# Attention routing on a second PSUM bank and at other places, states stored in another order, and eight zero products per iteration

## The chip, the cores and the metric

The kernel runs on one core of a Trainium2 chip. The metric is the device time of one execution in microseconds. Five engines work side by side, each through its own list of instructions in order: PE (TensorE, with its weight loads shown as PEld), DVE (VectorE), ACT (ScalarE), POOL (GpSimd) and SP (which here only issues DMAs). They wait for one another through semaphores.

## The reference

Three layers in a row. The first is a gated linear attention over 4 batches, 8 heads, 768 positions and a head size of 48, the second a top-1 mixture of 8 experts over the resulting 3072 tokens, the third a gated feed-forward layer:

```
for t in range(S):
    state = alpha[:, :, t, :, None] * state + k_t (outer) v_t
    y[:, :, t] = q_t @ state
logits = x @ w_gate;  expert = argmax(logits)
out[token] = gate[token] * (relu(x @ w1[expert]) @ w2[expert])
h = out @ w_in;  result = (h * sigmoid(h)) @ w_out
```

## The kernel before

**Attention.** Two heads of a batch form a pair; there are 16 pairs (0 to 15), four to a batch, and the main loop runs over the pairs `p`, one iteration each, and once more for the tail of the last pair. The 768 positions are cut into 6 chunks of 128. In iteration `p` PE computes, in this order:

- the scores of pair `p` (`scores`, tile Ap, PSUM banks 0 and 1);
- transposes of the scaled keys (`ks_transpose`, tile Tp, bank 2), four chunks, and two more later; ACT copies each lot out to kst;
- the part of the output of pair `p - 1` that comes from its states (`from_states`, tile Yp, banks 5 and 6), which reads the states So;
- the chunk updates of the state (`updates`, tiles U in bank 3 and, for half chunks, Ue in bank 4);
- between the two the part of the output within a chunk (`within`, into Yp).

DVE runs two long decay scans (Pf at L570, Rv at L588), masks the scores (Am, L621), scales the keys (L593), and in `states` scans U into the running states (run, L654) and adds Ue into So (L664); ACT copies the rest of So (L663). `from_states` of the next iteration needs both.

**Routing.** When the four pairs of a batch are done, the tokens of that batch are routed beside the following pairs. The steps are: the gate's logits (Lp), a turn (Lt), the choice of an expert and its weight (small DVE steps), ranks within the expert (`ranks`, pp), slots, six turned blocks of rows (`rows`, tile Xt: four PE transposes, then two ACT activations at L955 that scale by the gate weight into xr, and every second block a store to DRAM), and the inverse list (`hots` on DVE, `invert`, tile pt, on PE, `add` on DVE). All PSUM tiles of the routing come from `xbank()`, which in the attention gives bank 7 and only that; each of them therefore waits until the one before it has been read out.

**What sets the order.** The program is written under a manual schedule: each engine runs its instructions in the order in which the code issues them. `aside(p, place)` issues the routing steps that a hand-written table (`beside_pairs`) has put at a place of iteration `p`. The places in order are A (behind the scores), F1 and F2 (ahead of `from_states`), F3 (behind the second lot of key transposes), U (ahead of the updates), C1 (behind `states`) and C2. Routing of batch 0 lies beside pairs 5 to 10, that of batch 1 beside 9 to 14, that of batch 2 beside 13 to 15, and that of batch 3 behind the attention, beside the first expert tiles.

**Warming.** In iterations 0 to 4 some products on a tile of zeros (`warm`, tile Lw, L543, 256 columns each) run on PE beside the real ones; later iterations have none.

**Behind the attention** come the expert products and the last layer, where PE runs without a pause.

Of the kernel before, what the change touches and what calls it, by code (L numbers as in the profile page):

```python
# [23 lines left out]
PA = 112  # L24
CH = 128
# [215 lines left out]
def gla_moe_kernel(  # L241
# [164 lines left out]
    with actx:  # L406
# [127 lines left out]
        constants()  # L534
        U = bank(3, [PA, D, NC], "U")
        nc.vector.memset(U, 0.0)
        Ue = bank(4, [PA, NC, D], "Ue")
        nc.vector.memset(Ue, 0.0)
        Lw = bank(7, [128, 256], "Lw")

# [96 lines left out]
        def updates(p, n):  # L637
            s = st[p]
            for c in range(NC - 1 if n == CH else NC):
                for h in range(2):  # L640
                    r = slice(64 * h, 64 * h + D)
                    nc.tensor.matmul(
                        U[r, :, c + 1] if n == CH else Ue[r, c, :],
                        lhsT=s["kst"][:n, c, r],
                        rhs=s["v"][:n, (h * NC + c) * D : (h * NC + c + 1) * D],
                        start=True,
                        stop=True,
                    )

        def states(p):  # L650

            so = So[p % 2]
            run = wk.tile([PA, D, NC], F32, tag="run", name="run")
            nc.vector.tensor_tensor_scan(  # L654
                run.rearrange("p e c -> p (e c)"),
                U.rearrange("p e c -> p (e c)"),
                st[p]["W"],
                0.0,
                op0=ALU.add,
                op1=ALU.mult,  # L660
            )
            by_c = run.rearrange("p e c -> p c e")
            nc.scalar.copy(so[:, D:NS].rearrange("p (c e) -> p c e", e=D), by_c[:, 1:NC])  # L663
            nc.vector.tensor_tensor(so[:, NS : 2 * NS].rearrange("p (c e) -> p c e", e=D), by_c, Ue, op=ALU.add)  # L664

        xb = {}

# [4 lines left out]
        def from_states(p):  # L672

            s = st[p]
            s["y"] = y = [bank(5 + h, [128, NC, HC], "Yp") for h in range(2)]
            new = set()
            for c in range(NC):
                for u in range(2):
                    for h in range(2):
                        if c or u:  # L680
                            r, z = slice(64 * h, 64 * h + D), slice(u * HC, u * HC + HC)
                            o, w = half(h, u), (u * NC + c) * D
                            s["mm"] = nc.tensor.matmul(
                                y[h][o : o + 64, c, :],
                                lhsT=So[p % 2][r, w : w + 64],
                                rhs=s["qs"][r, c, z],
                                start=(h, u) not in new,
                                stop=False,
                            )
                            new.add((h, u))  # L690
# [37 lines left out]
        XB = [0]  # L728

        XBS = [7]  # L730

        def xbank():
            XB[0] += 1
            return XBS[XB[0] % len(XBS)]

# [255 lines left out]
        def beside_pairs(b):  # L991
            s_, tb = route(b)
            digits, hots, invert, add = tb
            row = [lambda c=c: rows(b, c) for c in range(NC)]
            p = 4 * b + 5
            at = {
                (p, "A"): [lambda: logits(b), s_["l_copy"]],
                (p, "F2"): [s_["l_turn"]],
                (p, "F3"): [s_["l_rows"], *s_["choose"][:2], s_["w_exp"]],
            }  # L1000
            if b < B - 2:
                at |= {
                    (p, "C1"): s_["choose"][2:] + [s_["w_gate"]],
                    (p + 1, "F2"): [s_["ranks"]],
                    (p + 1, "C1"): s_["slots"],
                    (p + 1, "C2"): [digits],
                    (p + 2, "F2"): [row[0]],
                    (p + 2, "F3"): [row[1]],
                    (p + 3, "F1"): [row[2]],
                    (p + 3, "F2"): [row[3]],  # L1010
                    (p + 3, "F3"): [row[4]],
                    (p + 4, "F1"): [row[5], hots],
                    (p + 5, "F1"): [invert, add],
                }
            else:
                at |= {
                    (p, "C1"): s_["choose"][2:] + [s_["w_gate"]],
                    (p + 1, "A"): [row[0], row[1]],
                    (p + 1, "F2"): [row[2]],
                    (p + 1, "F3"): [s_["ranks"], lambda: w_cast(2), lambda: w_cast(3)]  # L1020
                    + s_["slots"]
                    + [digits, lambda: w_rest(2), row[3], row[4]],
                    (p + 1, "U"): [row[5]],
                    (p + 1, "C1"): [hots],
                    (p + 2, "F2"): [invert, add, gather_a],
                    (p + 2, "C2"): [lambda: w_cast(0), lambda: w_cast(1), lambda: w_rest(3), lambda: w_rest(0), lambda: w_load(4)],
                }
            return at

        def aside(p, place):  # L1030
            for step in plan_r.get((p, place), []):
                step()
# [23 lines left out]
        for p in range(NP + 1):  # L1056
            on, oy = p < NP, p >= 1
            if on:
                begin(p)
                scores(p)  # L1060
            if p == 0:
                for t in [So[i][:, 2 * NS :] for i in range(2)] + [Es[NE][32:64]]:
                    nc.gpsimd.memset(t, 0.0)
            prepare(p, "head")

            aside(p, "A")
            if on:
                ks_transpose(p, 0, 4)
                if beside_scans(p):
                    mask_aside(p)  # L1070
            if p % 4 == 1 and 1 < p < NP:
                gather_last(p // 4)
            prepare(p, "scan")
            aside(p, "F1")
            if 1 <= p <= 4:
                warm(3)
            aside(p, "F2")
            if oy:
                from_states(p - 1)
            if on:  # L1080
                ks_transpose(p, 4, NC)
            else:
                st[p - 1]["mark"] = behind(nc.scalar.copy(wz[:, 0:1], wz[:, 1:2]), st[p - 1]["mm"])
            aside(p, "F3")
            if p == 0:
                warm(8)
            for T, i in work.get((p, "scan"), []):
                f(T, Q_SCALE)
                f(T, DECAY)
            aside(p, "U")  # L1090
            if not on:
                x_rows(XG[0], XS[0], 0, 0, 128, bank(2, [128, KD, 128], "xt"))
                x_rows(XG[1], XS[0], 1, 0, CA - 128, bank(0, [128, KD, 128], "xt"))
                w_rest(1)
            if on:
                updates(p, CH)
            if oy:
                within(p - 1)
            if oy:
                y_copy(p - 1, 0)  # L1100
                y_copy(p - 1, 1)
            if on:
                updates(p, HC)
                states(p)
            if p == 0:
                warm(22)
            aside(p, "C1")
            prepare(p, "end")
            if p == 1:
                nc.gpsimd.memset(wgs, 0.0)  # L1110
            if p == 2:
                for h in range(2):
                    for u in range(2):
                        z = wgs[half(h, u) : half(h, u) + D, h].rearrange("p i x -> p (i x)")
                        src = wg[64 * h : 64 * h + D].rearrange("p i x -> p (i x)")
                        nc.sync.dma_start(z[:, u * E :], src[:, 0 : 4 * 32 - u * E])
            if p == 5:
                more_constants()
            aside(p, "C2")
            if 1 <= p <= 3:  # L1120
                warm(3)
            if not on:
                logits(B - 1)
                last, last_tb = route(B - 1)
                last["l_copy"]()
                for t in range(5, 8):
                    w_load(t)
            if p + 1 in loads:
                load(loads[p + 1], "a")
            if p:  # L1130
                load_v(p + 2)
            if p + 1 in loads:
                load(loads[p + 1], "qk")
            if p >= 4 and p % 4 == 0 and p < NP:
                for at, todo in beside_pairs(p // 4 - 1).items():
                    plan_r[at] = plan_r.get(at, []) + todo
            if p in (11, 12):
                for t in range(2):
                    w_load(2 * (p - 11) + t)
# [591 lines left out]
```

## Time and profile before

| what | value |
| --- | --- |
| time, median of 3 runs | 796.06 us (795.36 to 797.17) |
| time of the profiled execution | 793.69 us |
| its span | 791.9 us |
| mean granted TensorE clock | 0.952 of full |
| busy share of PE, DVE, ACT, POOL | 96%, 59%, 45%, 19% |

The span is what the profile covers; the profiled execution's own time is 1.8 us longer. The attention lies in the first fifth of the span, so shares over the whole span say little about it; it has to be read by stretches of time. A granted clock of 1.00 is 2.4 GHz and of 0.50 is 1.2 GHz; values between are mixtures of the two in one stretch.

### The profile page before, as it was taken

The page shows a single profiled execution, that of the slowest core. Times are in us where ns is not written, and L with a number is a line of the kernel's source. Part 1 is how long each engine was busy: PE and PEld are TensorE (multiplying, and loading weights), DVE is VectorE, ACT ScalarE, POOL GpSimd, SP SyncE. Part 2 cuts the span into 40 slices and gives each one's busy share as a digit, 9 for nine tenths or more (in the row PEclk, how much of TensorE's full clock was granted, in tenths as well). Part 3 has the DMA queues.
Part 4 walks back from the last instruction along what each step waited for, and adds up shares of the span by engine and source line. Part 5 has one row for each costly group of instructions (what it writes and reads, how often), then busy time and mean ns, then how long its engine had stood idle before and what let it go on. Part 6 is the DMA issues. An engine that isn't in the chain of part 4 may idle for free. (4 is left out here: it accounts for less than half of the span.)

```text
span 791.9 us, 16908 instructions
## 1 busy us (share of the span) xinstructions
PE 756.9 (96%) x6730; PEld 692.2 (87%) x6730; DVE 468.4 (59%) x784; ACT 359.8 (45%) x691; POOL 152.4 (19%) x204
## 2 busy tenths in 40 slices
PE   8889787899999999999999999999999999999997
PEld 6668675779999999999998998989988999898996
DVE  8977775455678778888878533442333333344322
ACT  2334354343555554666644424554454545244222
POOL 5443341113043332311112120020010002002002
PEclk9976778588999999999999999999999999999999
DMA  9686974444366557666320120022012001001001
GB/s 247 166 204 173 218 218 111 110 107 154 126 193 192 177 173 205 198 185 190 122 81 21 36 75 18 1 75 52 3 38 72 19 18 41 2 0 41 1 1 43
DMA packets 41944, 81.25 MB, mean 103 GB/s; under 512 B 5840, under 2 KB 20127, under 8 KB 41832
## 3 DMA queue, kind: packets, MB, share of 16 engines
q1 hardware_dynamic: 37832, 67.64, 29.8%
q0 software_dynamic: 4000, 12.03, 5.1%
q8 instruction: 81, 1.33, 0.7%
q14 instruction: 31, 0.25, 0.1%
HBM read 68.08 MB, written 9.47 MB: 98 GB/s over the span
## 5 line engine op out<-in xcount | busy, mean ns | idle before, releaser
L1252 PE MATMUL hp<-xh,wh 128*128 128x512 f32 (+10 forms) x498 | 181.4, 366 | 1.0 <-ACT xh L378 1.0
L1252 PE MATMUL hp<-xh,wl 128*128 128x512 f32 (+10 forms) x498 | 180.9, 365 | 0.0
L1526 DVE TENSOR_TENSOR sg<-hp,sg 128x512 f32<-128x512 f32 (+1 forms) x97 | 66.5, 685 | 128.1 <-ACT sg L1525 127.6
L1252 PE MATMUL hp<-xl,wh 128*128 128x512 f32 (+10 forms) x498 | 127.4, 364 | 0.0
L1525 ACT ACTIVATE sg<-hp 128x512 f32<-128x512 f32 (+1 forms) x97 | 57.5, 593 | 118.1 <-PE hp L1252 113.3
L1252 PEld LDWEIGHTS hp<-xh,wh 128*128 128x128 f32 x498 | 94.7, 190 | 12.9 <-PE Lp L740 1.2
L1252 PEld LDWEIGHTS hp<-xh,wl 128*128 128x128 f32 x498 | 94.8, 190 | 10.5
L1252 PEld LDWEIGHTS hp<-xl,wh 128*128 128x128 f32 x498 | 90.5, 189 | 11.8
L1571 POOL DMA_INDIRECT out_dram<-o,sidx x24 | 23.3, 973 | 275.6 <-ACT o L1569 271.1
L1179 POOL TENSOR_TENSOR wl<-dx,wh 128x384 fp32r<-128x384 f32 x32 | 39.5, 1234 | 165.3 <-ACT wh L1176 165.3
L346 DVE TENSOR_TENSOR wl<-raw,wh 128x768 fp32r<-128x768 f32 x64 | 65.3, 1024 | 7.2 <-ACT wh L342 6.6
L1290 ACT ACTIVATE hh<-hp 128x464 fp32r<-128x464 f32 (+9 forms) x70 | 34.0, 487 | 75.3 <-PE hp L1252 68.4
L1292 DVE SCALAR_TENSOR_TENSOR hl<-hp,hh 128x464 fp32r<-128x464 f32 (+9 forms) x70 | 38.0, 549 | 29.8 <-ACT hh L1290 29.5
L1537 DVE TENSOR_TENSOR hl<-sg,hh 128x512 fp32r<-128x512 f32 x49 | 33.9, 692 | 35.9 <-ACT hh L1536 34.5
L342 ACT CAST wh<-raw 128x768 fp32r<-128x768 f32 x64 | 51.9, 832 | 6.1 <-DMA raw<-in_wt_dram 5.8
L1536 ACT CAST hh<-sg 128x512 fp32r<-128x512 f32 x49 | 30.4, 621 | 50.1 <-DVE sg L1526 38.4
L1537 DVE TENSOR_TENSOR xl<-sg,xh 128x512 fp32r<-128x512 f32 (+1 forms) x48 | 32.7, 681 | 31.7 <-ACT xh L1536 21.3
L1342 PE MATMUL both<-hh,wh 128*128 128x396 f32 (+9 forms) x140 | 47.8, 341 | 0.0
L1342 PE MATMUL both<-hl,wh 128*128 128x396 f32 (+9 forms) x140 | 46.1, 329 | 0.1
L1342 PE MATMUL both<-hh,wl 128*128 128x396 f32 (+9 forms) x140 | 45.9, 328 | 0.0
L1536 ACT CAST xh<-sg 128x512 fp32r<-128x512 f32 (+1 forms) x48 | 29.3, 611 | 35.1 <-DVE sg L1526 32.0
L364 POOL DMA_INDIRECT xg<-x_d,gidx x29 | 33.4, 1152 | 54.2 <-PE hp L1252 23.6
(335 smaller groups left out, 1580.4 us busy)
## 6 DMA issues: line engine op xcount, KB each, us to landing
raw<-in_wt_dram SPq DMA_DIRECT2D x64, 384.0 KB
raw<-in_w_dram SPq DMA_DIRECT2D x32, 384.0 KB
raw<-in_alpha_dram SPq DMA_DIRECT2D x16, 336.0 KB
x_d<-xr SPq DMA_DIRECT2D x24, 192.0 KB
E<-in_q_dram SPq DMA_DIRECT2D x18, 144.0 KB
E<-in_k_dram SPq DMA_DIRECT2D x18, 144.0 KB
E<-E POOLq DMA_DIRECT2D x18, 114.0 KB
E<-in_q_dram SPq DMA_DIRECT2D x4, 336.0 KB
```

The costliest lines, as they stand in the source:

```text
L342: nc.scalar.copy(wslot[slot1(t)][0], raw[t])
L346: eng.tensor_tensor(lo, raw.pop(t), hi.bitcast(F32), op=ALU.subtract)
L364: nc.gpsimd.indirect_dma_start(out=x[:n], out_offset=None, in_=src, in_offset=bass.IndirectOffsetOnAxis(ap=idx[:n, i : i + 1], axis=0),)
L1179: nc.gpsimd.tensor_tensor(r["lo"], r["x"], r["hi"].bitcast(F32), op=ALU.subtract)
L1252: nc.tensor.matmul(hp, lhsT=a[:, kc * 128 : (kc + 1) * 128], rhs=x[:, kc, c0:c1], start=(i == 0), stop=(i == 8))
L1290: nc.scalar.activation(hh[:, :n], hp, AF.Relu)
L1292: nc.vector.scalar_tensor_tensor(hl[:, :n], in0=hp, scalar=0.0, in1=hh[:, :n].bitcast(F32), op0=ALU.max, op1=ALU.subtract)
L1342: nc.tensor.matmul(yb[dc][:, c0:c1], lhsT=a[:, c : c + 128], rhs=b_[:, : c1 - c0], start=(f == 0 and c0 == 0 and i == 0), stop=(f == NF - ...
L1525: nc.scalar.activation(sg[:, z], hp[:, z], AF.Sigmoid)
L1526: nc.vector.tensor_tensor(sg[:, z], hp[:, z], sg[:, z], op=ALU.mult)
L1536: nc.scalar.copy(hh[:, z], sg[:, z])
L1537: nc.vector.tensor_tensor(hl[:, z], sg[:, z], hh[:, z].bitcast(F32), op=ALU.subtract)
```

## The change

Three things are edited.

1. `lent` is a list of banks that `xbank()` hands out first. The table puts `two(2)`, which lends bank 2 (that of the key transposes Tp), ahead of some steps at place U. The table itself puts the row blocks, `ranks`, `l_turn`, `hots`, `invert` and `add` at other places; a place C0, right behind `states`, is new.
2. Ue is laid out with the chunk innermost, as U is. `states` now reads run in its own order and writes So with a step of 48 numbers, where before it read run with a step of 6 numbers and wrote So in order. What So holds and how `from_states` reads it is as before.
3. `from_states` issues eight products of 128 x 128 on the tile of zeros, into columns of bank 5 that nothing else uses, ahead of its own products. It runs 16 times.

```diff
-        Ue = bank(4, [PA, NC, D], "Ue")
+        Ue = bank(4, [PA, D, NC], "Ue")
...
-                        U[r, :, c + 1] if n == CH else Ue[r, c, :],
+                        U[r, :, c + 1] if n == CH else Ue[r, :, c],
...
-            by_c = run.rearrange("p e c -> p c e")
-            nc.scalar.copy(so[:, D:NS].rearrange("p (c e) -> p c e", e=D), by_c[:, 1:NC])
-            nc.vector.tensor_tensor(so[:, NS : 2 * NS].rearrange("p (c e) -> p c e", e=D), by_c, Ue, op=ALU.add)
+            nc.scalar.copy(so[:, D:NS].rearrange("p (c e) -> p e c", e=D), run[:, :, 1:NC])
+            nc.vector.tensor_tensor(so[:, NS : 2 * NS].rearrange("p (c e) -> p e c", e=D), run, Ue, op=ALU.add)
...
-            s["y"] = y = [bank(5 + h, [128, NC, HC], "Yp") for h in range(2)]
+            t = [bank(5 + h, [128, 512], "Yp") for h in range(2)]
+            s["y"] = y = [x[:, 0 : NC * HC].rearrange("p (c t) -> p c t", c=NC) for x in t]
+            for _ in range(8):
+                nc.tensor.matmul(t[0][:, NC * HC :], lhsT=wz[:, 0:128], rhs=wz[:, 0:128], start=True, stop=True)
...
+        lent = []
...
+            if lent:
+                return lent.pop(0)
             XB[0] += 1
             return XBS[XB[0] % len(XBS)]
...
-                (p, "F2"): [s_["l_turn"]],
-                (p, "F3"): [s_["l_rows"], *s_["choose"][:2], s_["w_exp"]],
+                (p, "F3"): [s_["l_turn"], s_["l_rows"], *s_["choose"][:2], s_["w_exp"]],
...
+            two = lent.append
...
-                    (p + 2, "F2"): [row[0]],
-                    (p + 2, "F3"): [row[1]],
-                    (p + 3, "F1"): [row[2]],
-                    (p + 3, "F2"): [row[3]],
-                    (p + 3, "F3"): [row[4]],
-                    (p + 4, "F1"): [row[5], hots],
-                    (p + 5, "F1"): [invert, add],
+                    (p + 2, "A"): [row[1]],
+                    (p + 2, "F3"): [row[2]],
+                    (p + 2, "U"): [lambda: two(2), row[3]],
+                    (p + 3, "A"): [row[4]],
+                    (p + 3, "F3"): [row[5]],
+                    (p + 4, "F1"): [hots],
+                    (p + 4, "U"): [lambda: two(2), invert],
+                    (p + 4, "C0"): [add],
...
+            aside(p, "C0")
             aside(p, "C1")
```

What this makes of PE's list in iteration 14 (beside which batch 2 is routed) is shown here. Xt x8 are two row blocks, x12 three; pt is `invert`, pp `ranks`, Yp at L683 `from_states`. Before, from the scores of pair 14 to its first updates:

```order
L616 MATMUL Ap<-E_139 64x64 x24
L944 MATMUL Xt<-ident,xb 128x112 x8
L603 MATMUL Tp<-ident,E_139 128x112 x4
L886 MATMUL pt<-rv,ol 128x32 x6
L944 MATMUL Xt<-ident,xb 128x112 x4
L683 MATMUL Yp<-E_138,So_172 64x64 x22
...
L944 MATMUL Xt<-ident,xb 128x112 x12
L642 MATMUL U<-v__2251,kst 48x48 x10
```

And in the change (`from_states` is at L685, the row blocks at L949, the zero products at L677):

```order
L616 MATMUL Ap<-E_139 64x64 x24
L949 MATMUL Xt<-ident,xb 128x112 x4
L603 MATMUL Tp<-ident,E_139 128x112 x4
L949 MATMUL Xt<-ident,xb 128x112 x4
L677 LDWEIGHTS wz
L677 MATMUL Yp<-wz 128x128
...
L685 MATMUL Yp<-E_138,So_172 64x64 x22
...
L949 MATMUL Xt<-ident,xb 128x112 x4
L642 MATMUL U<-v__2356,kst 48x48 x10
```

Of six row blocks ahead of the updates of pair 14 three are left; the others follow `states` and go into iteration 15, and `invert` of batch 1 has moved to iteration 13.

The second place is iteration 12 on PE, beside which rows of batch 1 are turned. Before:

```order
L616 MATMUL Ap<-E_137 64x64 x24
L603 MATMUL Tp<-ident,E_137 128x112 x4
L944 MATMUL Xt<-ident,xb 128x112 x8
L683 MATMUL Yp<-E_142,So_172 64x64 x22
L603 MATMUL Tp<-ident,E_137 128x112 x2
L944 MATMUL Xt<-ident,xb 128x112 x4
L642 MATMUL U<-v__1949,kst 48x48 x10
```

And in the change:

```order
L616 MATMUL Ap<-E_137 64x64 x24
L949 MATMUL Xt<-ident,xb 128x112 x4
L603 MATMUL Tp<-ident,E_137 128x112 x4
L677 LDWEIGHTS wz
L677 MATMUL Yp<-wz 128x128
...
L685 MATMUL Yp<-E_142,So_172 64x64 x22
L603 MATMUL Tp<-ident,E_137 128x112 x2
L949 MATMUL Xt<-ident,xb 128x112 x4
L642 MATMUL U<-v__2037,kst 48x48 x10
```

Where two blocks stood one behind the other ahead of `from_states`, one now stands ahead of the key transposes and one behind `from_states`, and the third has gone to iteration 11.

## Rows read from the trace of the kernel before

**Rows 1.** The page, the span in 40 slices: PE's busy tenths and granted clock.

```profile
PE   8889787899999999999999999999999999999997
PEclk9976778588999999999999999999999999999999
```

**Rows 2.** Windows by stage: length, busy per engine, clock, DMA share, GB/s.

```profile
10.00:161.50 151.50, 126.77 (x3271) 103.33 (x3269) 109.69 (x165) 63.52 (x146) 47.43 (x64) 0.78 0.68 178
200.00:787.40 587.40, 586.33 (x3120) 547.69 (x3118) 328.13 (x534) 278.29 (x504) 86.45 (x98) 1.00 0.26 80
```

**Rows 3.** Windows by iteration, 6 to 15: length, PE, PEld, DVE, ACT, POOL, clock, DMA.

```profile
56.00:65.00 9.00, 7.10 (x201) 6.13 (x199) 5.72 (x13) 3.09 (x8) 1.63 (x1) 0.73 0.81 204
65.00:74.00 9.00, 9.00 (x204) 8.12 (x202) 7.34 (x11) 4.16 (x10) 4.82 (x5) 0.51 0.71 182
74.00:80.70 6.70, 5.77 (x214) 5.09 (x210) 6.36 (x7) 4.62 (x13) 0.49 (x1) 1.00 0.50 129
80.70:88.70 8.00, 7.09 (x223) 5.09 (x219) 7.32 (x12) 3.89 (x11) 4.11 (x7) 1.00 0.90 205
88.70:101.20 12.50, 9.04 (x211) 8.21 (x207) 5.88 (x14) 3.00 (x8) 1.63 (x1) 0.59 0.91 232
101.20:107.50 6.30, 5.79 (x211) 4.82 (x205) 5.95 (x9) 3.27 (x9) 3.17 (x4) 1.00 0.63 186
107.50:118.00 10.50, 8.74 (x198) 7.70 (x200) 8.08 (x10) 5.87 (x15) 4.21 (x4) 0.68 0.79 226
118.00:126.20 8.20, 7.28 (x224) 5.29 (x220) 7.02 (x11) 3.48 (x9) 1.99 (x5) 0.99 0.80 195
126.20:144.30 18.10, 12.71 (x231) 10.55 (x227) 5.87 (x21) 8.73 (x22) 1.00 (x1) 0.65 0.32 82
144.30:154.20 9.90, 7.85 (x208) 6.90 (x204) 5.04 (x11) 3.36 (x8) 2.03 (x2) 0.67 0.31 91
```

**Rows 4.** Waits from 38 to 161 us: total, times, longest.

```profile
DVE run L654 <- PE U L642: 14.7, 8, 4.2
DVE So L664 <- PE Ue L642: 10.7, 10, 1.7
PE Xt L944 <- ACT xr L955: 6.4, 5, 2.0
PE Ap L616 <- issue: 2.5, 1, 2.5
```

**Rows 5.** Timeline of iterations 10, 12, 14: start, length, instruction, idle before.

```profile
95.94 0.20 PE L812 MATMUL pp<-oh,tri 128*128 128x48 bf16 x1 [0.96 <-DVE tab L892]
...
111.22 0.98 PE L944 MATMUL Xt<-ident,xb 112*128 112x112 f32 x4 [1.76 <-ACT xr L955]
...
129.73 0.60 PE L944 MATMUL Xt<-ident,xb 112*128 112x112 f32 x4 [1.97 <-ACT xr L955]
```

**Rows 6.** Groups of DVE by form: count, total us, mean ns, idle before.

```profile
L664 DVE TENSOR_TENSOR So<-run,Ue 112x288 f32<-112x288 f32 x16 | 10.9, 684 | 11.3 <-PE Ue L642 10.7
...
L573 DVE RECIPROCAL D<-Pf 128x6 f32<-128x6 f32 x9 | 1.7, 194 | 0.3
...
L781 DVE TENSOR_TENSOR oh<-w,fi 128x48 bf16<-128x48 f32 x3 | 1.0, 320 | 0.1
...
L836 DVE RECIPROCAL gt<-sm 128x6 f32<-128x6 f32 x4 | 0.8, 192 | 0.1
...
L775 DVE TENSOR_TENSOR eq<-eq,w 128x48 f32<-128x48 f32 x3 | 0.6, 208 | 0.1
...
L379 DVE TENSOR_TENSOR xl<-xt,xh 128x384 fp32r<-128x384 f32 x1 | 0.6, 557 | 1.1 <-ACT xh L378 1.1
```

**Rows 7.** Products into U and Ue in iteration 8: ns min/median/max, first and last start.

```profile
L642 PE MATMUL U<-v__1297,kst x20: 208/208/243, 78.9 to 79.4; 128*48 128x48 f32 x20
```

```profile
L642 PE MATMUL Ue<-v__1297,kst x24: 202/205/205, 80.2 to 80.7; 64*48 64x48 f32 x24
```

**Rows 8.** Timeline of the warming products of iteration 0.

```profile
15.04 2.58 PE L543 MATMUL Lw<-wz 128*128 128x256 bf16 x22
```

More of the change, by code (lines that the diff above doesn't have):

```diff
@@ L1003, in beside_pairs @@
                     (p, "C1"): s_["choose"][2:] + [s_["w_gate"]],
-                    (p + 1, "F2"): [s_["ranks"]],
+                    (p + 1, "F1"): [s_["ranks"]],
+                    (p + 1, "U"): [lambda: two(2), row[0]],
                     (p + 1, "C1"): s_["slots"],
                     (p + 1, "C2"): [digits],
-                    (p + 2, "F2"): [row[0]],
-                    (p + 2, "F3"): [row[1]],
-                    (p + 3, "F1"): [row[2]],
-                    (p + 3, "F2"): [row[3]],
-                    (p + 3, "F3"): [row[4]],
-                    (p + 4, "F1"): [row[5], hots],
-                    (p + 5, "F1"): [invert, add],
+                    (p + 2, "A"): [row[1]],
[6 more added lines that the diff above has]
+                    (p + 4, "C0"): [add],
                 }
@@ L1017, in beside_pairs @@
                     (p, "C1"): s_["choose"][2:] + [s_["w_gate"]],
-                    (p + 1, "A"): [row[0], row[1]],
-                    (p + 1, "F2"): [row[2]],
+                    (p + 1, "A"): [row[0]],
+                    (p + 1, "F2"): [row[1]],
                     (p + 1, "F3"): [s_["ranks"], lambda: w_cast(2), lambda: w_cast(3)]
                     + s_["slots"]
[L1022 to L1025, printed above, removed]
+                    + [digits, lambda: w_rest(2)],
+                    (p + 1, "U"): [lambda: two(2), row[2]],
+                    (p + 1, "C1"): [row[3], hots],
+                    (p + 2, "A"): [row[4]],
+                    (p + 2, "F2"): [row[5]],
+                    (p + 2, "F3"): [invert, add, gather_a],
                     (p + 2, "C2"): [lambda: w_cast(0), lambda: w_cast(1), lambda: w_rest(3), lambda: w_rest(0), lambda: w_load(4)],
```

## The prediction, made before the changed kernel was run

> **What bounds the kernel now.** I read the page's slices first [rows 1]: PE is at nine tenths from the ninth slice on, but its clock is below full in slices 3 to 10. So there are two stages. From 200 us on PE is busy 586.33 of 587.40 us at full clock [rows 2]; nothing of the change lies there, and what the attention gains or loses arrives at the end as it is. From 10 to 161.5 us PE is busy 126.77 us at a mean clock of 0.78 and DVE 109.69 us [rows 2]: neither is full, they wait for each other. The waits say how [rows 4]: DVE waited 14.7 us for the updates U and 10.7 us for Ue. DVE has its scans done and PE is late.
>
> The windows by iteration show when [rows 3]. At full clock an iteration takes 6.30 us (11), 6.70 (8), 8.00 (9) or 8.20 (13), and DVE is busy in 6 to 7 us of it: there DVE is the bound. Iteration 7, at 0.51 of the clock throughout, takes 9.00 us with PE busy in all of it: there PE is the bound. Three are longer: 10 with 12.50 us, 12 with 10.50 and 14 with 18.10, all with DVE below 8.1 us and a clock of 0.59 to 0.68. Ahead of each lies a PE pause: a wait of 2.5 us inside the scores of iteration 10 for nothing that the profile shows [rows 4], and 1.76 and 1.97 us in which row blocks wait until ACT has read the block before out of bank 7 [rows 5]. The clock then stands at half for several us.
>
> **The change part by part.**
>
> Row blocks and bank 2, iterations 14 and 15. Before, six blocks, `invert` and `ranks` use bank 7 one behind the other ahead of the updates of 14, and DVE stands 4.2 us for U [rows 4]. Now three blocks stand there, one of them on bank 2. What is left: iteration 11 with its two blocks is the model at full clock, 6.30 us [rows 3]. To it I add one wait, since the second block still waits until ACT has scaled the first, which waits for the gate weight (1.97 us before [rows 5], I take 1.5 as one block now lies ahead of it and not two), one more block (0.60 us [rows 5]), and the zero products (0.7, below): 9.1 us. At half clock I scale the model by 9.00 to 6.70, iteration 7 to iteration 8 [rows 3]: 11.2 us. So iteration 14 gains 6.9 to 9.0 us; I take 7.5. Iteration 15 takes over three blocks, 1.8 us and a wait or two for ACT between them, but has `invert` behind `from_states` and no longer ahead of it, and DVE is free there for 4.9 us (9.90 less 5.04 [rows 3]): +2 at half clock to -2 at full; I take -0.5.
>
> Iterations 10 and 12. In 10, `invert` of batch 0 and the 0.96 us for which `ranks` waited on DVE behind it [rows 5] go to iteration 9; a block comes in ahead of U: about -1 net, -5 if the 2.5 us pause does not come back and the clock stays up (12.50 against 8.00 with a margin). I take -2. In 12 the 1.76 us wait goes, and with it the clock's fall behind it: the iteration should come near DVE's 8.08 us of work [rows 3], -2 of a possible 2.4; the lower bound is 0, if the clock falls for another reason.
>
> What the moves cost elsewhere. `invert` now lies ahead of U in 9 and 13, on bank 2, behind `hots` on DVE: about 0.8 us for PE, by what iterations 9 and 13 (8.00 and 8.20 us long, DVE busy 7.32 and 7.02 [rows 3]) can hide 0.7 to 1.2; I take +0.5 each. Behind the waiting instruction stand U and then the scan into run on DVE. Blocks at U in 6, 7, 10, 11 and 14 must wait for ACT's copy of the second key lot out of bank 2. At U one block at full clock is 0.60 us, at half 0.98 [rows 5]; in 6 and 7 the clock is low and DVE waits, so up to 2 us are seen, while blocks no longer stand ahead of `from_states` there. I put 6 and 7 together at +0.5. Stores of the rows move with the blocks on SP's queue; the loads queued behind them have the DMA engines at 0.31 to 0.91 of their time [rows 3], and I cost this at nothing while an iteration of lead remains; without it, the loads set the pace (a rival below).
>
> States. DVE's add into So takes 684 ns for 288 elements [rows 6]; the nearest addition that reads PSUM and has everything in order is 384 elements in 557 ns [rows 6], which gives 0.42 us for 288 by proportion, or 0.46 if the 0.19 us of a 6-element row [rows 6] is what an instruction costs at any size. Now the reads are in order and the writes step by 192 bytes. Rows with stepped writes: the one-hot list, 48 numbers of two bytes, takes 320 ns against 208 in order, 2.3 ns an element more; the reciprocal of 6 four-byte numbers, which steps in reading and in writing, 194 ns against 192 [rows 6]. The first would make 0.45 + 288 x 0.0023 = 1.11 us, the second 0.45. Element size is the likelier kin, so I take a part of the gain, 0.15 of a possible 0.23 us, seen in some ten iterations where DVE is the bound or on the way from Ue to the next step: -1.5 us; bounds -3.7 and +6.8 (16 x 0.43).
>
> Ue's products now write PSUM with a step of six numbers. U's products already do so: 208 ns each against 205 for Ue, and 20 of them start within 0.5 us as 24 do [rows 7]. That is at most 5 ns a product, 0.1 us an iteration, behind `within`; I take 0.
>
> The Trainium skill, "SBUF — State Buffer", section "Door 1: The DMA port swizzle", says that PSUM has lines of two fp32 values and that any pattern out of order slows matmuls significantly. The trace does not agree: the U row is out of order by six numbers and shows 208 ns.
>
> Zero products. The warming products of 256 columns come at (2.58 - 0.27) / 21 = 0.11 us each, taking 0.27 as one's own length, an estimate from [rows 8]. Eight of half the columns cost 0.44 to 0.88 us at full clock, at most 1.76 at half. They stand where PE often waits for So, so where DVE is the bound they are hidden by that wait, and they fill pauses ahead of which the clock fell. In PE-bound iterations (5, 6, 7, 10) they are paid: 4 x 0.7 = 2.8 us, less what the clock gives back; I take +1 net. They also fetch 256 more instructions, and pauses such as the 2.5 us [rows 4] will lie elsewhere; I cost that at 0.
>
> Behind the attention the gather of the first rows now follows the last store of batch 2 more closely: +0.5.
>
> The sum: -7.5 - 0.5 - 2 - 2 + 1 + 0.5 - 1.5 + 1 + 0.5 = -10.5 us. The profiled execution took 793.69 us, so 783.2; it lies 2.4 us below the median of the runs, 796.06, from which the same sum gives **785.6 us**. A measurement of this kernel tells about 0.2%, 1.6 us, from no change.
>
> **The rivals.**
>
> The clock stays up. If the zero products and the shorter waits keep PE at full clock from 46 us on, iterations 6 to 15 come down to DVE's work or the 6.3 to 8.2 us of the full-clock ones [rows 3]: 6 and 7 give 4, 10 gives 4.5, 12 gives 2.5, 14 and 15 give 10, the states 1.5: some 22 us, 774. For it: every fall follows a PE pause. Against it: 2.5 us of pause is not the routing's, and 0.7 us of zeros is less than the pauses. Chance 0.18.
>
> Only the worst knot is untied. DMA engines are busy 0.71 to 0.91 in iterations 6, 7, 9, 10, 12 and 13 [rows 3]; if loads then set the pace, or the clock falls as before, only iteration 14 gains, and zeros and blocks ahead of U eat half of it: -1 to -5, 791 to 795. Chance 0.12, half of it within 0.2%.
>
> Slower: the zero products are paid in full. If they do not lift the clock, cost 1.76 us at half clock and lie on the path in iterations 5 to 7, 10, 12 and 14 to 16, that is 14 us against the +1 of the sum: -10.5 + 13 = +2.5, 798.6. It decides from about 1.4 us an iteration in these eight. Against it: PE waits for So just there. Chance 0.10 (with stepped writes at 1.11 us, which alone would bring the sum to -2).
>
> Products out of order in PSUM slow down. If Ue's 24 products, which now take 0.7 us from the first start to the last end [rows 7], took twice that, 16 iterations would give +11 and the sum +0.5: 796.6. The U row speaks against it. Chance 0.02.
>
> This is what the Trainium skill's page "SBUF — State Buffer", cited above, would make of the change.
>
> **How the numbers follow.** My forecast, -6 to -15 us, has 0.58, so 785.6 is its middle. The range reaches down into the rival with the full clock, 772, and up to the untied knot, 793.5; above lie 0.18, below some 0.02. Faster by over 0.2%: 0.58 + 0.18 + 0.07 = 0.83; within: 0.07; slower: 0.10.
>
> **What would show it.** Iteration 14 of about 9 to 11 us; no wait of Xt for xr above 1 us in iteration 12; DVE's add into So between 0.45 and 0.68 us; DVE's wait for U below 7 us in all; the zero products within 0.9 us of PE at full clock; Ue's products still at 205 to 210 ns. I am wrong if the add takes over 0.7 us, if zero products stand on the path at half clock, or if DVE or POOL waits for loads.

## The result and the profile after

| | kernel before | change |
| --- | --- | --- |
| first comparison, median | 795.71 us (4 runs) | 788.53 us (4 runs, 783.51 to 797.73) |
| ratio | | 0.9895, 95% interval 0.9854 to 0.9936 |
| profiled execution, its span, mean granted clock | 793.69 us, 791.9 us, 0.952 | 790.69 us, 789.0 us, 0.969 |
| second comparison, in a later session | 791.48 us (34 runs) | 791.18 us (12 runs), ratio 1.003 (0.9996 to 1.0063) |
| third comparison, on another chip than the second | 791.89 us (17 runs) | 791.19 us (12 runs), ratio 0.9986 (0.9950 to 1.0023) |

Ratios, unlike medians, leave out runs more than 1.5% above the fastest of their kernel: here one of the change's four (797.73 us, with which the two means stand at 0.993), below four of e10's twelve and the profiled executions of e6, e8 and e12, whose profiles are not used. The first comparison says about 1% faster, close to the predicted 785.6 us. The two later ones, with many more runs, show no change: their intervals reach from 0.995 to 1.006. The change stands at 788.5 to 791.2 us each time; what moved more is the kernel before, from 795.7 to 791.5. The chip of the first comparison is not on record. So the gain of the first comparison is not confirmed, and the larger part of this study asks where the gain that the prediction added up has gone.

The page's slices of the change, PE's busy tenths and the granted clock; slices 3 to 5, 7 and 8, which stood at 8 to 5 tenths [rows 1], have more clock now, and none has less:

```profile
PE   8879798789999999999999999999999999999997
PEclk9997979888999999999999999999999999999999
```

Windows by iteration, 6 to 15, cut at the first row of each iteration's scores; columns as in [rows 3]:

```profile
54.35:67.82 13.47, 9.40 (x215) 8.08 (x211) 5.70 (x13) 3.59 (x9) 3.37 (x17) 0.62 0.91 199
67.82:74.88 7.06, 6.33 (x222) 5.62 (x218) 6.49 (x10) 3.65 (x10) 3.46 (x5) 1.00 0.69 192
74.88:80.83 5.95, 5.85 (x214) 5.27 (x210) 5.84 (x6) 4.14 (x12) 1.38 (x1) 1.00 0.74 188
80.83:90.68 9.85, 7.71 (x232) 6.04 (x229) 8.46 (x14) 3.73 (x9) 4.60 (x7) 1.00 1.00 204
90.68:102.90 12.22, 8.66 (x214) 7.15 (x211) 5.70 (x14) 3.80 (x10) 1.62 (x1) 0.67 0.79 181
102.90:111.73 8.83, 8.71 (x217) 7.82 (x215) 7.22 (x11) 4.54 (x12) 4.81 (x5) 0.68 0.73 202
111.73:117.32 5.59, 5.59 (x215) 5.15 (x210) 5.29 (x5) 3.38 (x9) 0.00 (x0) 1.00 0.83 245
117.32:128.11 10.79, 9.07 (x234) 7.13 (x229) 8.27 (x14) 4.07 (x10) 4.57 (x7) 0.88 0.91 241
128.11:137.49 9.38, 7.57 (x227) 6.63 (x224) 5.68 (x22) 6.39 (x16) 0.99 (x1) 0.95 0.23 50
137.49:144.80 7.31, 6.69 (x213) 6.06 (x213) 3.99 (x10) 3.76 (x11) 0.00 (x0) 1.00 0.51 123
```

The reader is to see both signs. Iteration 14 takes 9.38 us (18.10 in [rows 3]) and 12 takes 5.59 (10.50). But 9 takes 9.85 (8.00), 11 takes 8.83 (6.30), 13 takes 10.79 (8.20), and 6 takes 13.47 (9.00).

The waits of the change from 38 to 157 us (total, times, longest), those that answer to [rows 4] and two new ones:

```profile
DVE run L654 <- PE U L642: 10.3, 5, 4.7
...
DVE So L663 <- PE Ue L642: 7.2, 9, 1.7
...
PE xt L374 <- DMA xg<-x_d,gidx_a: 4.9, 1, 4.9
PE Ap L616 <- issue: 4.5, 2, 3.6
...
PE pt L891 <- DVE ol L886: 3.0, 2, 1.7
...
PE Yp L685 <- issue: 2.6, 1, 2.6
...
PE Xt L949 <- ACT xr L960: 1.9, 2, 1.4
```

The wait of row blocks for ACT fell from 6.4 to 1.9 us. New are 4.9 us for the first gathered rows behind the attention and 3.0 us in which the inverse list waits for DVE. "issue" is time that nothing in the profile explains; in the scores it was 2.5 us and is 4.5.

**Where the new places gain and lose.** One profile of each kernel isn't enough, since the pauses put down to "issue" lie elsewhere in each execution. The experiments below gave four profiles of the routing as before (the kernel before, e3, e7, e11) and seven of the new routing (the change, e1, e2, e4, e5, e9, e10). Lengths of iterations in us, from the first row of the scores to the next one's, mean (lowest to highest):

```
iteration        routing as before      new routing           difference
6                9.0  (6.9 to 11.0)     10.0 (7.4 to 13.5)    +1.0
7                8.1  (5.9 to 9.2)       7.2 (6.7 to 8.0)     -0.9
8                7.9  (6.7 to 10.7)      6.5 (5.6 to 9.6)     -1.4
9                8.5  (8.0 to 9.8)      10.2 (9.3 to 12.0)    +1.7
10              12.2 (11.4 to 12.5)      9.9 (5.6 to 13.0)    -2.3
11               6.1  (5.8 to 6.3)       7.8 (6.6 to 9.0)     +1.7
12              10.5  (9.2 to 11.1)      6.0 (5.6 to 6.9)     -4.5
13               8.2  (8.0 to 8.5)      11.2 (9.4 to 12.4)    +3.0
14              18.5 (18.0 to 19.5)     11.4 (9.3 to 13.3)    -7.2
15 to first hp  15.9 (13.4 to 17.8)     19.1 (17.1 to 20.0)   +3.2
```

"First hp" is the first expert product. In 11, 12, 13 and 14 the two sets don't overlap: one execution's pauses don't make them; in 9 and behind 15 they overlap little. The gains of 10, 12 and 14 are 14.0 us, the losses of 9, 11, 13 and behind 15 are 9.6.

The total of the rows, -5.7 us, is not the gain of the kernel. The seven profiled executions took 787.1 us in the mean and the four 792.5, which is 5.4 less; those of e1, e2 and e5 were the shortest of their kernel's twelve runs. The single rows tell where time moved; how much is left of it is told by the ratios.

**The inverse list.** Timeline of the change in iteration 13 (start, length, instruction, idle before):

```profile
121.86 0.94 DVE L593 TENSOR_TENSOR E<-E,Rv 128x768 f32<-128x768 f32 x1
...
122.72 0.34 DVE L884 TENSOR_TENSOR eqh<-iota_f,hi 128x192 f32<-128x192 f32 x1
...
123.10 0.36 DVE L885 TENSOR_TENSOR rv<-eqh,tokid 128x192 fp32r<-128x192 f32 x1
...
123.38 0.95 DVE L886 TENSOR_TENSOR ol<-iota_f,lo 128x768 fp32r<-128x768 f32 x1
...
124.47 0.81 PE L891 MATMUL pt<-rv,ol 128*128 128x32 f32 x6 [1.72 <-DVE ol L886]
...
125.22 0.81 PE L642 MATMUL U<-v__2203,kst 128*48 128x48 f32 x20
...
125.96 1.55 PE L712 MATMUL Yp<-Am,v__2037 64*64 64x64 f32 x48
...
126.14 0.76 DVE L654 TENSOR_TENSOR_SCAN run<-U,E 112x288 f32<-112x288 f32 x1 [1.06 <-PE U L642]
```

`hots` stands on DVE behind the scaling of the keys (L593), so its last tile `ol` is there at 124.33, while PE has been free since 122.75. The inverse list stands ahead of the updates, so U comes 1.72 us plus its own 0.8 us late, DVE in turn waits 1.06 us for U, and `within` then takes 1.55 us at half clock (0.89 at full in iteration 12). No run moved `invert` back by itself, so that this is what iterations 9 and 13 lost is argued from the timeline, not tested. Up to the start of iteration 15 the wait for `ol` is 2.3 to 3.2 us in all in the new-routing profiles where nothing fills it, and nothing in those of the routing as before, where these two inverse lists stood an iteration later (0.4 us, for ACT). The row of the kernel before:

```profile
PE pt L886 <- ACT xr L955: 0.4, 1, 0.4
```

**The gather.** The same view behind the attention:

```profile
143.07 0.17 DVE L970 TENSOR_SCALAR gidx_a<-tab 128x2 uint32<-128x2 f32 x1
...
145.83 1.36 POOL L364 DMA_INDIRECT xg<-x_d,gidx_a  x1 [12.20 <-DVE So L663]
...
147.50 0.93 POOL L364 DMA_INDIRECT xg<-x_d,gidx_a  x1 [0.31 <-issue]
...
151.43 0.62 PE L374 MATMUL xt<-identr,xg 128*128 128x128 f32 x3 [4.92 <-DMA xg<-x_d,gidx_a]
```

And in the kernel before:

```profile
148.08 0.17 DVE L965 TENSOR_SCALAR gidx_a<-tab 128x2 uint32<-128x2 f32 x1
...
148.54 1.09 POOL L364 DMA_INDIRECT xg<-x_d,gidx_a  x1 [15.56 <-DVE fl L966]
...
155.65 0.63 PE L374 MATMUL xt<-identr,xg 128*128 128x128 f32 x3
```

In the change the step that makes the indices starts at 143.07 and the rows can be turned at 151.43. Two things differ from before. The gather starts 2.76 us behind the start of the index step, where it started 0.46 us behind it. The trace's DMA packets show what it waits for: those of the last row store end at 144.44 us, behind the indices, and the gather starts 1.39 us after that; before, they end at 145.14 us, 2.9 us ahead of the indices. It is so in all eleven: the gather starts 1.4 to 1.6 us behind the last store in the seven profiles of the new routing, 0.46 us behind the index step in the four others. And iteration 15 took 9.90 us [rows 3], so that PE didn't wait for these rows; now it takes 7.31 us, ends at 144.80, and PE stands. The stretch behind, 149.40 to 156.30 us, has a clock of 0.51.

The wait is not the whole of what is lost there. From iteration 15 to the first expert product e2 has no wait for rows, is at half clock throughout with PE busy, and takes as long as any:

```profile
130.90:150.92 20.02, 19.94 (x335) 15.66 (x334) 7.56 (x14) 7.78 (x18) 2.03 (x2) 0.50 0.47 135
```

**States and zero products.** The group of the addition, Ue's products in iteration 7 and one iteration's zero products:

```profile
L663 DVE TENSOR_TENSOR So<-run,Ue 112x288 f32<-112x288 f32 x16 | 10.6, 663 | 9.0 <-PE Ue L642 8.5
```

```profile
L642 PE MATMUL Ue<-v__1185,kst x24: 202/205/217, 74.4 to 74.9; 64*48 64x48 f32 x24
```

```profile
132.25 0.61 PE L677 MATMUL Yp<-wz 128*128 128x128 bf16 x8
```

The addition takes 663 ns (684 in [rows 6]), Ue's products 205 ns as in [rows 7], eight zero products 0.61 us with the last one's own 0.22 us, so by estimate one each (0.61 - 0.22) / 7 = 0.056 us.

### The profile page after: what moved, and what is told of

It reads as the page before. It is cut to its first block, busy times and chain, and to the rows that moved or that the text cites. A ratio compares the mean times of both kernels' runs of the same rounds, so it can differ in the third digit from the quotient of the medians.

```text
span 789.0 us, 17156 instructions
## 1 busy us (share of the span) xinstructions
PE 753.3 (95%) x6858; PEld 691.4 (88%) x6858; DVE 466.0 (59%) x784; ACT 358.0 (45%) x691; POOL 151.2 (19%) x204
## 5 line engine op out<-in xcount | busy, mean ns | idle before, releaser
L342 ACT CAST wh<-raw 128x768 fp32r<-128x768 f32 x64 | 51.8, 831 | 10.5 <-DMA raw<-in_wt_dram 10.3
```

What stands on the lines that cost most here:

```text
L342: nc.scalar.copy(wslot[slot1(t)][0], raw[t])
```

## The experiments

All ratios are to the kernel before on the same chip, with 95% intervals. e1 to e4 ran on one chip beside 33 runs of the kernel before (median 790.51 us), e5 to e8 on the same chip beside 34 (791.48 us), e9 to e11 on another beside 29 (794.13 us), e12 on a third beside 17 (791.89 us). "Time by clock" in some expectations is the time multiplied by the mean granted clock, a rough account only, as it counts a wait spent at half clock as half.

**e1_no_zeros: the change without the zero products.**

```diff
-            for _ in range(8):
-                nc.tensor.matmul(t[0][:, NC * HC :], lhsT=wz[:, 0:128], rhs=wz[:, 0:128], start=True, stop=True)
```

> The changed kernel without its zero products. Theory 1 (they pay: they keep the clock up in the attention): the mean granted clock falls from 0.97-0.98 back to about 0.955-0.965 and the time lies 2 to 5 us above the changed kernel, about 0.993-0.996 of the kernel before. Theory 2 (they cost: 16 x 0.55 us on the path and more pauses of PE that the profile explains by nothing): the clock stays, the pauses on PE in the attention come down from 10.7 us to the 5.9 us of before, and the time lies 2 to 6 us below the changed kernel.

Ratio 1.0025 (0.9982 to 1.0068), median 794.52 us. With them (e5) it is 1.003: no difference that can be told. The mean clock is 0.961 without and 0.966 with them, as the first expectation had it, but the time moves neither way clearly. PE waits for So 1.8 us in all without them, so most of their 16 x 8 x 0.056 = 7.2 us cannot have been hidden in that wait.

**e2_old_states: the change with Ue and So in the order of before.**

```diff
-        Ue = bank(4, [PA, D, NC], "Ue")
+        Ue = bank(4, [PA, NC, D], "Ue")
...
-            nc.scalar.copy(so[:, D:NS].rearrange("p (c e) -> p e c", e=D), run[:, :, 1:NC])
-            nc.vector.tensor_tensor(so[:, NS : 2 * NS].rearrange("p (c e) -> p e c", e=D), run, Ue, op=ALU.add)
+            by_c = run.rearrange("p e c -> p c e")
+            nc.scalar.copy(so[:, D:NS].rearrange("p (c e) -> p c e", e=D), by_c[:, 1:NC])
+            nc.vector.tensor_tensor(so[:, NS : 2 * NS].rearrange("p (c e) -> p c e", e=D), by_c, Ue, op=ALU.add)
```

> The changed kernel with Ue and the writing of So as before. In the changed kernel's profile DVE's add into So takes 663 ns against 684 before and ACT's copy 630 against 640, so the new order should be worth at most 16 x 0.02 = 0.3 us: the time of this kernel equals the changed kernel's within 1 us. Rival (the forecast's term): 1.5 us or more above it.

Ratio 1.0012 (0.9975 to 1.0050), median 790.51 us; the addition takes 686 ns. No difference to the change that can be told.

**e3_zeros_only: the kernel before with the eight zero products.** The edit is that part of the change alone.

> The kernel before with the eight zero products alone. Theory 1 (they lift the clock): mean clock from 0.952 to 0.96 or more, 2 to 5 us below the kernel before. Theory 2 (they cost): 0 to 5 us above it, with pauses of PE of 8 us or more in the attention. The long wait in iteration 14 (18 us long) stays in both.

Ratio 1.0071 (1.0032 to 1.0111), median 796.82 us: slower. Windows of the attention up to the first expert product, of this kernel:

```profile
10.00:161.70 151.70, 126.05 (x3398) 104.54 (x3398) 107.56 (x165) 63.34 (x146) 49.35 (x64) 0.85 0.68 175
```

In this profile the attention is as long as before (151.50 us [rows 2]) at a clock of 0.85 instead of 0.78. But it is of an execution of 789.59 us, 7.2 below the median. Over the ten runs the mean clock is 0.963, beside 0.962 for the kernel before, and the time by clock 765.6 us beside 760.0: the products cost most of the 7.2 us that they take, and the clock gives nothing back.

**e4_rows_behind: the change with the turning of the first gathered rows moved behind the last logits.**

```diff
-                x_rows(XG[0], XS[0], 0, 0, 128, bank(2, [128, KD, 128], "xt"))
-                x_rows(XG[1], XS[0], 1, 0, CA - 128, bank(0, [128, KD, 128], "xt"))
...
                 last["l_copy"]()
+                x_rows(XG[0], XS[0], 0, 0, 128, bank(2, [128, KD, 128], "xt"))
+                x_rows(XG[1], XS[0], 1, 0, CA - 128, bank(0, [128, KD, 128], "xt"))
```

> The changed kernel, in which the transposes of the first gathered rows stand behind the last products of the attention and the last logits. In the changed kernel's profile PE stands 4.9 us for the gather ahead of them and has 4.3 us of such products behind them. Theory (the end of the attention is set by the chain from the last row store of batch 2 through the gather, which the change exposed): the wait falls below 1 us and the first expert product comes 3 to 4 us earlier, 0.984 to 0.987 of the kernel before. Rival (the time is set elsewhere, by the routing of batch 3 and its weights): within 1 us of the changed kernel.

Ratio 1.0004 (0.9972 to 1.0036), median 790.14 us. The wait, which was to fall below 1 us, is 3.3 us instead of 4.9 and 0.3, and the stretch to the first expert product, 17.1 us, is the shortest of the seven. A gain of 1 to 2 us would fit, but it can't be told from the change.

**e5_after_again: the change unedited.**

> The changed kernel unedited, once more against the kernel before, because the kernel before took 790.5 us in the median of 33 runs beside the first experiments and 795.7 us beside the change, and three relatives of the change that keep all of its routing came out at 1.0004 to 1.0025 of it. Theory (the gain of iteration 14 is real and not eaten elsewhere): ratio 0.985 to 0.993. Rival (the 7 us of the first comparison are where PE's pauses and the clock's falls happened to lie in four runs of each kernel, and what iteration 14 gives is paid back behind the attention and in zero products): ratio 0.997 to 1.003, about 790 us.

Ratio 1.003 (0.9996 to 1.0063), median 791.18 us: the rival.

**e6_routing_only: the new places and the second bank alone** (e1 and e2 together).

> Only the routing's new places and its second bank; no zero products, and the states read and written as before. Theory: it carries the whole gain, iteration 14 takes 9 to 11 us as in the change, and the time is that of the change or up to 3 us below it. By the zero products put alone into the kernel before (ratio 1.007), it should be some 3 to 5 us faster than the change. Rival: it stands within 0.3% of the kernel before, because PE waits 4 to 5 us for the first gathered rows behind the attention whatever the rest does.

Ratio 0.9983 (0.9938 to 1.0027), median 793.59 us. The new places don't gain what the prediction gave them, with or without zero products.

**e7_states_alone: the kernel before with the states in the new order.** The edit is that part of the change alone.

> Only the states in the other order on the kernel before. Theory: the addition into So takes 0.66 us instead of 0.68, so at most 16 x 0.02 = 0.3 us are to be had: ratio 0.998 to 1.002. Rival, that of the prediction: some ten additions on the way to the next step give 1.5 us, ratio 0.998 or below. If Ue's products slowed in PSUM, their 205 ns would rise and the ratio go over 1.005.

Ratio 0.9993 (0.9963 to 1.0024), median 789.95 us; the addition takes 658 ns. By its own length that is worth 16 x 0.026 = 0.4 us at most.

**e8_zeros_16: the change with sixteen zero products.**

```diff
-            for _ in range(8):
+            for _ in range(16):
```

> The change with sixteen zero products per iteration instead of eight. Theory: zero products are paid where PE is the bound and shift when DVE's next step starts, 0.3 to 0.6 us an iteration more for each eight: 3 to 6 us over the change. Rival: they stand in a wait for So or buy back as much by the clock, and the time stays within 0.3% of the change with a mean granted clock that is higher by 0.005 or more.

Ratio 0.9986 (0.9948 to 1.0023), median 791.96 us. Over the runs that the ratios use, none, eight and sixteen products (e6, e5, e8; the states of e6 are those of before, which e7 shows to matter nothing) give a mean granted clock of 0.960, 0.966 and 0.978, and 788.9, 791.7 and 789.9 us in the mean: the clock rises with each eight, the time doesn't move. Time by clock is 757.5, 764.4 and 772.6 us: each eight costs about the 7.2 us that they take, and the clock gives it back. Of the two expectations the rival holds.

**e9_waits_filled: e6 with idle transposes of the identity right ahead of four instructions that wait** (10 and 14 ahead of the inverse list in 9 and 13, 40 ahead of the first gathered rows, 14 ahead of the second expert tile).

```diff
-                r["pt"] = bank(bk(), [128, nhi], "pt")
+                t = bank(bk(), [128, 256], "pt")
+                r["pt"] = t[:, 0:nhi]
+                for _ in range({0: 10, 1: 14}.get(b, 0)):
+                    nc.tensor.transpose(t[:, 128:256], ident, ident)
...
+        for _ in range(fill):
+            nc.tensor.transpose(t[:, 0, :].bitcast(F32R), identr, identr)
```

> Routing only (no zero products ahead of the states' part, states as before), but with idle transposes of the identity put right ahead of four instructions on which PE waits anyway: 10 and 14 ahead of the inverse list in iterations 9 and 13, 40 ahead of the first gathered rows behind the attention, 14 ahead of the second expert tile's rows, at about 0.11 us each at full clock. Routing only gave 792.0 us in the mean at a mean granted clock of 0.955, and time multiplied by clock was 756.6 us, 3.1 us below the kernel before. Theory (the clock falls behind PE's pauses, and what stands in a wait costs nothing): time by clock stays at 756 to 759 us and the clock rises to 0.967 or more, 780 to 784 us, ratio 0.986 to 0.992. Rival (the falls come as often wherever PE's list has no such work, and the mean clock settles where it was): 790 to 793 us.

Ratio 0.9922 (0.9889 to 0.9954), median 786.80 us, mean clock 0.974. PE's waits of this kernel, and two windows behind the filled places:

```profile
PE xt L376 <- DMA xg<-x_d,gidx_a: 2.1, 1, 2.1
PE hp L1266 <- ACT xh L380: 2.1, 1, 2.1
```

```profile
150.00:157.00 7.00, 6.93 (x101) 5.19 (x101) 3.26 (x11) 2.98 (x9) 0.00 (x0) 1.00 0.19 59
...
175.00:186.00 11.00, 10.83 (x84) 10.83 (x85) 5.26 (x13) 4.61 (x11) 3.25 (x4) 0.84 0.23 78
```

Behind the gather PE runs at 1.00, where the change had 0.51. The ratio is just above the theory's range; the account behind it is not what was expected, since time by clock rose to 766.8 us (756 to 759 expected): the 78 fillers are not free, but the clock pays for them and for some more.

**e10_filled_behind: the change with the two fillers behind the attention.** The edit is the second part of that of e9, on the change.

> The change, with its eight zero products per iteration, and besides 40 idle transposes ahead of the first gathered rows and 14 ahead of the second expert tile's rows. Theory: the two half-clock stretches that followed these waits in the profile of the change (149.4 to 156.3 and 173.3 to 183.6 us) go, some 3 to 8 us: 784 to 789 us, clock 0.970 or more against 0.964. Rival: within 0.3% of the change unedited.

Ratio 0.9921 (0.9881 to 0.9961), median 791.91 us, mean clock 0.978. The ratio agrees with the theory, and the second and third ratio of the change unedited lie above its interval; but the medians differ by 0.3% only and the means of all runs by 0.5%, so not much rests on it.

**e11_before_filled_tile: the kernel before with 14 idle transposes ahead of the second expert tile's rows.**

> The kernel before with only 14 idle transposes ahead of the second expert tile's rows, where PE waited 1.52 us for gathered rows and the clock stood at half from 179.6 to 186.4 us. Theory: time by clock unchanged at 760 us, the stretch behind stays at full clock, 2 to 4 us faster, ratio 0.995 to 0.998. Rival: ratio 0.999 to 1.002, with the half-clock stretch in the profile as before or elsewhere.

Ratio 1.0011 (0.9977 to 1.0044), median 794.11 us: the rival. In the kernel before PE does pause here, behind the attention, and stands at half clock after it:

```profile
178.01 0.43 PE L374 MATMUL xt<-identr,xg 128*128 128x128 f32 x3 [1.52 <-DMA xg<-x_d,gidx]
```

```profile
179.60:186.40 6.80, 5.80 (x29) 5.52 (x28) 1.95 (x6) 1.18 (x3) 2.83 (x4) 0.50 0.67 213
```

Timeline of PE and windows with the fillers:

```profile
178.94 1.33 PE L374 MATMUL xt<-identr 128*128 128x128 f32 x14
...
181.11 0.45 PE L376 MATMUL xt<-identr,xg 128*128 128x128 f32 x3 [0.83 <-DMA xg<-x_d,gidx]
...
185.29 0.39 PE L376 MATMUL xt<-identr,xg 64*128 64x64 f32 x3 [1.40 <-issue]
...
186.82 0.34 PE L1254 MATMUL hp<-xh,wh 128*128 128x232 f32 x1 [1.13 <-issue]
```

```profile
178.00:184.00 6.00, 5.06 (x48) 4.74 (x47) 3.07 (x11) 0.65 (x2) 4.49 (x5) 1.00 0.62 189
184.00:190.00 6.00, 3.57 (x21) 3.52 (x22) 2.21 (x9) 1.12 (x3) 2.11 (x3) 0.80 0.47 147
```

Behind the filled wait the clock stays at 1.00; it falls after two pauses of 1.40 and 1.13 us that nothing in the profile explains. In this execution what one place saves is lost at the next.

**e12_again: the change unedited, a third time.**

> The changed kernel unedited for a third time, because the kernel before took 790 to 791 us on the chip of the first eight experiments and 794 us on that of the last three, at the same product of time and clock (759.5 to 760 us) and a mean granted clock of 0.961 against 0.957. Theory (the change adds 4 to 7 us of time at full clock and gets them back by a clock of 0.965 to 0.975, so what it gains is set by how much the kernel before loses to the clock on the chip at hand): ratio 0.990 to 0.997 where the kernel before runs at 0.958 or below, 0.999 to 1.004 where it runs at 0.961 or above; time by clock 764 to 767 us in both cases. Rival (chance decides it and the change is worth nothing): time by clock as above, but the clock at 0.964 and the time at 791 to 793 us whatever the kernel before does.

Ratio 0.9986 (0.9950 to 1.0023), the kernel before at a mean clock of 0.961. Time by clock is 765.7 us and the mean clock 0.970. Clock and time by clock are the theory's case for such a chip, the ratio lies just outside its 0.999 to 1.004; the rival, whose time it meets as well, is not excluded.

## Why the prediction came out as it did

The number was close in the first comparison (788.53 against 785.6, inside the range), but the sum behind it was not right, and the later comparisons show the difference: that first closeness is largely luck. The mechanism of its main term was right; three costs, `invert`, the gather and the zero products, were sized far too small. The prediction also took a comparison to tell 0.2% from no change; the two later ones are uncertain by 0.3 to 0.4% each. In the order of the sum, beside the differences of the table:

- **Iteration 14, -7.5:** right, -7.2 in the mean and -8.7 in the two profiles. It takes 9.38 us in the change, as "9 to 11", and 11.4 in the mean of the seven. DVE's wait for U from 38 to 161 us is 3.5 to 10.3 us in the seven profiles, against 12.7 to 17.2 in the four.
- **Iteration 15, -0.5, and the gather, +0.5:** together +3.2. The gather term had the right mechanism and was mis-sized: the gather now waits for the last store, which puts it 0.97 to 4.34 us behind the index step instead of 0.46. What it left out is that the iteration which covers the way from index to rows had become shorter. In four of the five profiles where nothing fills it, PE stands 3.3 to 5.4 us for the rows; in the fifth, e2, half clock takes the same time.
- **Iterations 10 and 12, -2 each:** -2.3 and -4.5, with +1.7 in 11 to be set against them: one row block more stands there, and a clock that fell in 10 lasts into it (0.68). The wait for ACT in 12 has gone as said.
- **`invert` in 9 and 13, +0.5 each:** +1.7 and +3.0. This step failed. I counted PE's 0.8 us and what an iteration can hide, and priced nothing for the fact that `ol` is the last of three DVE steps behind the scaling of the keys; `hots` at F1 of the same iteration is too late for a place ahead of U. The wait itself is 1.72 us in 13, and half clock follows it.
- **Iterations 6 and 7, +0.5:** +1.0 and -0.9, right in the sum, though 6 depends on a pause of up to 3.6 us. Iteration 8, which has no term, gained 1.4, with overlap.
- **States, -1.5:** 0.4 at most (e7). I took the element size as the nearer kin and so a part of the gain; the stepped write of four-byte numbers costs nearly what the stepped read did.
- **Zero products, +1 net:** +5.6 us alone on the kernel before (e3, 0.0071 x 790.51), nothing that can be told in the change (e1 against e5). The claim that they stand in PE's wait for So failed: without them that wait is 1.8 us in all (e1), and in the trace of the kernel before, from 38 to 161 us, it was no longer:

```profile
PE Yp L683 <- DVE So L664: 1.4, 2, 0.9
```

  By time by clock they are paid at about their own length, 5 to 8 us, less than the 14 of the slower rival. In the change the clock gives about that back; on the kernel before it did not. Why it differs is open.
- **Ue's products, 0:** right, 205 ns before and after. The rule of the Trainium skill, "SBUF — State Buffer", section "Door 1: The DMA port swizzle", that a PSUM pattern out of order slows matmuls significantly, would have made the change slower; the rows don't agree with it.

Of what I said would show it, DVE's wait for U below 7 us was missed in the change (10.3) and met in e1 and e2. The sign I named as proof of error, POOL waiting for loads, is there (7.9 and 6.1 us for decay inputs), but waits of up to 9.2 us stand also in profiles of the routing as before (e3, e11), so they are not the change's. One sum is off by a hundredth: by its own terms the chances of faster and within are 0.82 and 0.08.

Adding the table's ten rows gives -5.7 us, while e5, e6 and e12 show -0.2 to +0.3%. That is hardly more than the 5.4 us by which the profiled executions of the seven were shorter, as said with the table. That iterations 11 to 14 changed is shown by profiles that don't overlap, and that nothing is left in the time by the ratios; what pays back the last few microseconds is not resolved.

**Left open.** Why the first comparison found 1%. Single runs of the change spread by 3.6 to 4.0 us and of the kernel before by 3.0 to 3.4 (standard deviations in the other comparisons), so a difference of two means of four is uncertain by some 2.4 us; 5.8 us were found over all eight runs, and chance is not excluded. The kernel before was at 795.7 us there and at 794.1 beside e9 to e11, where the two kernels with many fillers are 0.8% faster by their ratios; elsewhere it was at 790.5 to 791.9 us. That idle products pay where a chip grants the kernel before less clock (0.957 beside e9 to e11, 0.961 to 0.962 beside the others) fits these, but not e11, where 14 idle products gained nothing beside a clock of 0.957; and the change unedited was not run beside e9 to e11. e9 is the best candidate for a faster kernel, not shown beside the change on one chip.

## What to carry to other kernels

When a step is moved earlier, look at the engine that makes its input as closely as at the engine that runs it, and ask which transfers were hidden by the stretch that gets shorter, and which store they must wait for: the iterations where these stand lost 7.9 of the 14.0 us that were correctly found. Idle products that keep the clock up are not free even ahead of an instruction that waits; try them by dose, and judge by time, not by the clock. Four runs of each kernel can show 1% that two dozen in later comparisons don't, and the profiles of a few executions can add up to a gain that the runs don't have.

## What was unexpected of the hardware

- The kernel before has medians of 795.7, 790.5, 791.5, 794.1 and 791.9 us in five comparisons and runs from 783.0 to 801.7 us, with mean granted clocks of 0.957 to 0.962 in the comparisons of the experiments.
- None, eight and sixteen idle products per iteration gave mean granted clocks of 0.960, 0.966 and 0.978, and the time stayed within 0.4%.
- On DVE, 288 four-byte numbers written with a step of 192 bytes took 658 to 666 ns, the same read with a step of 24 bytes 680 to 686 ns.
- A gather of rows began 0.46 us behind the start of the step that makes its indices in the four profiles where the packets of the last row store had ended 2.8 us or more before that step, and 1.4 to 1.6 us behind those packets in the seven where they ended at most 0.4 us before it.
